# A dilated convolution with gates on one NeuronCore: short groups moved to the end, wide blocks re-spaced, preparation in smaller pieces

## The chip, the core and the metric

The kernel runs on one core of one Trainium2 chip. The metric is the time of one execution on the device in microseconds; the median of three runs of the kernel before is 282.95 (282.88 to 283.25). The engines of the core run their own queues side by side: TensorE (matmuls, PE in the profile), VectorE (DVE), ScalarE (ACT), GpSimd (POOL), and SyncE (SP), which here issues most transfers. Matmuls write to PSUM; GpSimd works on SBUF alone.

## The reference

```python
B, T, D, K = (2, 16000, 256, 3)
xp = jnp.pad(x, ((0, 0), (pad, 0), (0, 0)))      # dil = 2, pad = 4
h = jnp.einsum('btc,cd->btd', xp[:, pad:pad + T, :], w[0])
for i in range(1, K):
    off = pad - i * dil
    h = h + jnp.einsum('btc,cd->btd', xp[:, off:off + T, :], w[i])
f = h[..., :D].copy()
g = h[..., D:].copy()
z = jnp.tanh(f) * _sigmoid(g)
return z @ w_o
```

Each time step takes its input and those of 2 and 4 steps earlier through three 256 x 512 matrices; half of the result goes through tanh, half through a sigmoid, and their product through a 256 x 256 projection. Everything is bfloat16.

## The kernel before

**Rows and groups.** Four time steps make a row, so a batch has 4000 rows. A transposed load (L128) puts channels on the 128 partitions: `xt` holds, for each of the four steps of a row and for both halves of the channels, the rows side by side. Rows are cut into *groups* of R rows: 256 in most, and where a batch does not divide, 160 and 128 at its end (batch 0: 160 and 128; batch 1: 160, 128 and 128) and 128 at the start of batch 0. One or two groups share a loaded *chunk*. In the kernel before the groups stand batch after batch, so the two short ones of batch 0 are groups 12 and 13 of 28, in the middle.

**Blocks.** A group has four *blocks*, one for each 128 of the 512 output columns (`O_ORDER`; two for tanh, two for the sigmoid; `oi` is 0 to 3). The convolution is done with fewer products than its taps would need: sums and differences of inputs (`mm` L278, `pp` L284, `dd` L295) are multiplied with sums and differences of the weights (`wm`, `wp`, `wd`), four pairs of matmuls to a block (L314), and sums behind them (L348, L349) put the two halves right in the PSUM banks `a` and `b`.

**Wide blocks.** Three stretches of 256 rows in each batch go another way, with eight steps to a row and seven pairs of matmuls of 256 columns (L227) in place of four pairs of 512. That is less work for TensorE and more for the others: extra copies by ScalarE (L241, L242), four sums by VectorE (L247 twice, L257, L258), operands `qa`, `qb`, `qd` by GpSimd (L199, `wide_part`, six parts of 512 elements), `qp` (L214) and `qm` (L222). Six wide units of four blocks are put between the plain ones. They need three more weight matrices (`wf`, `wu`, `wt`), which VectorE makes in twelve steps (L571), and wide unit 0's operands, which GpSimd makes in twelve half parts ahead of it. The operands of unit n + 1 are made during the blocks of unit n (`Q_PARTS`).

**The order.** The order on every engine is written out: `slots` lists the 136 blocks, and the loop over k issues, for block k: on TensorE the first two products of block k, the last two of block k - 1, then projection pieces (`out_mm`, L413); on ScalarE the copy `ss` of one bank (L342), the eviction of earlier pieces (L450, L435) and the activations of block k - 1 (L372, L362); on VectorE the sums of block k, then one operation for `mm`, `pp` or a gate `zz` (L389), then what preparation is due; on GpSimd one part of `dd` for the next group, then a piece of the wide operands. `after` makes GpSimd's operations wait for VectorE's last one. For a wide block the products are `wide_first`, `wide_second` and `wide_last` (the last in block k + 1).

**Pieces.** A finished group's gated values go through the projection in *pieces* of four matmuls (`pieces`: 4 for a group of 256 rows or a wide unit, 3 for 160, of which one is a small `odd` one, 2 for 128). `drain` puts them on the list `todo`, from which each block takes one; behind the last wide block every second block takes two while there are more pieces left than blocks. A block that finds the list empty has none.

**Where the wide blocks stand** (the number is the block k; unit and `oi` run in order):

| | unit 0 | unit 1 | unit 2 | unit 3 | unit 4 | unit 5 |
|---|---|---|---|---|---|---|
| before | 40 43 46 49 | 63 66 69 72 | 75 78 81 84 | 87 90 93 96 | 99 102 105 108 | 111 114 117 120 |
| after | 34 36 46 52 | 57 60 63 66 | 69 71 75 78 | 81 83 86 89 | 92 95 98 101 | 104 106 109 112 |

Before, the weight steps are in blocks 9, 11, ... 31 and the half parts in 12, 14, ... 34; `qp` and `qm` of unit 0 in blocks 35 and 37. Short groups are blocks 52 to 59 and 124 to 135 before, 116 to 135 after.

Of the kernel before, what the change touches and what calls it, by code (L numbers as in the profile page):

```python
# [9 lines left out]
ALU = mybir.AluOpType  # L10
# [3 lines left out]
def kernel(  # L14
# [19 lines left out]
    nc = tc.nc  # L34
    bf16 = mybir.dt.bfloat16
    f32 = mybir.dt.float32
    B, T, D = x.shape
    K, _, D2 = w.shape
    P = 128
    assert K == 3 and D % P == 0 and D2 == 2 * D and T % 64 == 0  # L40
    CT = D // P
    NT = D // P
    RH = 16
    RG = 256
    N_WARM = 14
    O_ORDER = (0, 2, 1, 3)
# [2 lines left out]
    LAST = ((128,), (128, 128))  # L49
    N_DIRECT = 4  # L50
    N_WIDE = (3, 3)
    WIDE_FROM = 40
    PREP = 28
    W_FROM = 9
    EVERY = (2,)
    W_POOL = ()
    SUM_POOL = True
    GATE2 = False
    Q_PARTS = ((0, 1), ("s", 2), (3, 4), (5,))
    SPLIT_PROJ = 1  # L60
    W_STEP = 2
    P_STEP = 2
# [7 lines left out]


    groups, chunks, wides = [], [], []
    for b in range(B):
        r0 = 0
        wide = N_WIDE[min(b, 1)]
        head, tail = sizes(FIRST if b == 0 else (), LAST[min(b, 1)], wide)
        cuts = [1, 1] if b == 0 else []
        for rs in (head, tail):
            i = 0
            while i < len(rs):  # L80
                n = cuts.pop(0) if cuts else 2
                part = rs[i:i + n]
                chunks.append((b, r0, sum(part), len(groups), len(part)))
                for r in part:
                    groups.append(dict(wide=False, b=b, r0=r0, R=r, chunk=len(chunks) - 1, col=r0 - chunks[-1][1]))
                    r0 += r
                i += n
            if rs is head:
                assert r0 > 0 and r0 % 2 == 0
                for _ in range(wide):  # L90
                    wides.append(dict(wide=True, b=b, r0=r0, R=P))
                    r0 += RG
    XW = max(c[2] for c in chunks)

    consts = ctx.enter_context(tc.tile_pool(name="consts", bufs=1))
# [40 lines left out]
    w_taps = [consts.tile([P, CT, D2], bf16, name=f"w{k}_sb") for k in range(K)]  # L136
# [19 lines left out]
    wf_sb = consts.tile([P, CT, D2], f32)  # L156
    wu_sb = consts.tile([P, CT, D2], bf16)
    wt_sb = consts.tile([P, CT, D2], bf16)
# [24 lines left out]
            in_=x[G["b"], t0 - 8 * RH:t0 + 8 * P, :].rearrange("(r j) c -> r (j c)", j=8),  # L183
        )

    def wide_part(n, part, behind=None, qs=slice(0, 2)):

        G = wides[n]
        c = [G["x"][:, 2 * i:2 * i + 2, :, RH:RH + P] for i in range(4)]
        e = [G["x"][:, 2 * i:2 * i + 2, :, RH - 1:RH - 1 + P] for i in range(4)]  # L190
        if part == 0 and qs.start == 0:
            for nm in ("qa", "qb", "qd"):
                G[nm] = q_pool.tile([P, 2, 2, CT, P], bf16, name=nm)
        nm, h, in0, in1, op = (
            ("qa", 0, c[0], c[2], ALU.add), ("qb", 0, e[3], c[1], ALU.add),
            ("qa", 1, c[2], c[0], ALU.subtract), ("qb", 1, e[3], c[1], ALU.subtract),
            ("qd", 0, e[2], c[2], ALU.subtract), ("qd", 1, c[3], e[3], ALU.subtract),
        )[part]
        after(nc.gpsimd.tensor_tensor(out=G[nm][:, h, qs], in0=in0[:, qs], in1=in1[:, qs], op=op), behind)  # L199

    def gates(G):
        if GATE2 and G["R"] % P == 0:
# [6 lines left out]

    def wide_sum(n, behind=None):  # L210
        G = wides[n]
        G["qp"] = q_pool.tile([P, 2, CT, P], bf16, name="qp")
        eng = nc.gpsimd if SUM_POOL and behind else nc.vector
        ins = eng.tensor_tensor(out=G["qp"][:], in0=G["qa"][:, 0], in1=G["qb"][:, 0], op=ALU.subtract)  # L214
        if eng is nc.vector:
            return ins
        after(ins, behind)

    def wide_diff(n):
        G = wides[n]  # L220
        G["qm"] = q_pool.tile([P, 2, 2, CT, P], bf16, name="qm")
        return nc.vector.tensor_tensor(out=G["qm"][:], in0=G["qa"][:], in1=G["qb"][:], op=ALU.add)  # L222

# [6 lines left out]
            )  # L230

    def wide_first(G, oi):
        for bank, pool in (("a", ps_a), ("b", ps_b)):
            G[bank, oi] = pool.tile([P, 2 * RG], f32, name=bank)
        wide_mm(G, oi, wm_sb, G["qp"], "a", 1, True)
        wide_mm(G, oi, w_taps[1], G["qm"][:, 1], "a", 0)
        wide_mm(G, oi, wp_sb, G["qm"][:, 0], "b", 1, True)

    def wide_copies(G, oi):
        G["ss", oi] = ss_pool.tile([P, RG], f32, name="sw")  # L240
        nc.scalar.mul(G["ss", oi][:], G["a", oi][:, RG:], 0.5)  # L241
        nc.scalar.mul(G["a", oi][:, RG:], G["a", oi][:, :RG], -1.0)  # L242

    def wide_sums(G, oi):
        G["ud", oi] = ud_pool.tile([P, 2, RG], f32, name="ud")
# [5 lines left out]
    def wide_second(G, oi):  # L251
        wide_mm(G, oi, wt_sb, G["qa"][:, 1], "a", 0)
        wide_mm(G, oi, wu_sb, G["qb"][:, 1], "a", 1)
# [4 lines left out]
        nc.vector.tensor_tensor(out=G["a", oi][:], in0=ud, in1=G["a", oi][:], op=ALU.add)  # L258

    def wide_last(G, oi, bank):  # L260
        if bank == "b":
            wide_mm(G, oi, wd0_sb, G["qd"][:, 1], "b", 1)
        else:
            wide_mm(G, oi, wd2_sb, G["qd"][:, 0], "a", 0)

    def after(ins, behind):
        if behind is not None:
            tc.add_manual_dep(
                ins.ins, behind.ins.name,
                mybir.DependencyInfo(mybir.DependencyClass.Sync, mybir.DependencyReason.DATA),  # L270
                reason="GpSimd reads SBUF while VectorE's sums read PSUM",
            )
# [223 lines left out]
    NG = len(groups)  # L496
    plain = [(False, g, oi) for g in range(NG) for oi in range(4)]
    rest = [(True, n, oi) for n in range(len(wides)) for oi in range(4)]
    slots, since = [], 0
    for i, (_, g, oi) in enumerate(plain):  # L500
        slots.append(plain[i])
        since += 1
        full = all(groups[plain[j][1]]["R"] == RG for j in range(max(i - 2, 0), min(i + 2, len(plain))))
        if rest and i + 1 >= WIDE_FROM and since >= EVERY[(4 * len(wides) - len(rest)) % len(EVERY)] and full:
            slots.append(rest.pop(0))
            since = 0
    assert not rest
    NB = len(slots)
# [6 lines left out]
    todo, made = [], []  # L515
# [33 lines left out]
    for part in range(4):  # L549
        last = pre_d(1, part, nc.vector)  # L550
# [6 lines left out]
    drain(groups[0], N_DIRECT + 2)  # L557


    extra = {}  # L560
    last_wide = max(k for k in range(NB) if slots[k][0])
    first_wide = slots.index((True, 0, 0))

    def weight_steps(oi):
        o = O_ORDER[oi]
        osl = slice(o * P, (o + 1) * P)
        eng = nc.gpsimd if oi in W_POOL else nc.vector

        def tt(out, in0, in1, op):
            def step(last):  # L570
                ins = eng.tensor_tensor(out=out[:, :, osl], in0=in0[:, :, osl], in1=in1[:, :, osl], op=op)  # L571
                if eng is nc.vector:
                    return ins
                after(ins, last)
                return last
            return step

        return [
            tt(wf_sb, w_taps[2], w_taps[0], ALU.subtract),
            tt(wu_sb, wf_sb, w_taps[1], ALU.add),  # L580
            tt(wt_sb, wf_sb, w_taps[1], ALU.subtract),
        ]

    steps = [s for oi in range(4) for s in weight_steps(oi)]
    ks = [k for k in range(N_DIRECT + 2, NB) if not slots[k][0]]
    for kk, s in zip([kk for kk in ks if kk >= W_FROM][::W_STEP], steps):
        extra.setdefault(kk, []).append(s)

    load_wide(0)
    wides_loaded = 1  # L590
    wide_parts = {first_wide - PREP + P_STEP * i: divmod(i, 2) for i in range(12)}

    held = []
    filled = None
# [1 line left out]
    k = N_DIRECT + 1  # L596
    while k <= NB:
# [3 lines left out]
        if k < NB:  # L601
            if w:
                wide_first(G, oi)
                wide_copies(G, oi)
            else:
                products(k, 2)
                products(k, 1)
                copy_m2(k)
# [5 lines left out]
        if not prev["wide"]:  # L614
            products(k - 1, 3)
            products(k - 1, 0)
        if k < NB:
            for piece in made:
                out_evict(*piece, (not w and g == NG - 1 and oi in (0, 2)) or (len(made) > 1 and piece is made[1]))
            made = []  # L620
        second = (lambda: wide_second(G, oi)) if w else (lambda: wide_last(prev, poi, "b")) if prev["wide"] else None
        n = 0 if k in (NB - 2, NB - 1) else 2 if k > last_wide + 3 and k % 2 and unmade > NB - 1 - k else 1
        while todo and todo[0][0] <= k and n:
            piece = todo.pop(0)[1]
            out_mm(*piece, between=second)
# [51 lines left out]
        if k == last_wide + 2:  # L677
            last = gates(wides[-1])
            drain(wides[-1], k + 2)
        if k == first_wide - 5:  # L680
            last = wide_sum(0)
        if k == first_wide - 3:
            last = wide_diff(0)

        for step in extra.get(k, ()):
            last = step(last)
        if k < NB and g + 1 < NG:
            filled = last or filled
            if k + 1 < NB and slots[k + 1][0]:
                held.append(lambda last2, args=(g + 1, oi, nc.gpsimd), last1=last: pre_d(*args, last2 or last1))  # L690
            else:
                pre_d(g + 1, oi - 1 if g == 1 else oi, nc.gpsimd, last)
        if k in wide_parts:
            part, q = wide_parts[k]
            wide_part(0, part, last, slice(q, q + 1))
        if k < NB:
            activate(k - 1)
        if k < NB and oi == 3 and loaded < len(chunks) and groups[min(g + 1, NG - 1)]["chunk"] + 2 >= loaded:
# [3 lines left out]
                load_wide(1)  # L702
                wides_loaded = 2
        k += 1
    assert not todo, len(todo)
    finish(made)


# [28 lines left out]
```

## Time and profile before

| | us |
|---|---|
| median of three runs | 282.95 |
| profiled execution, its time | 282.88 |
| its span on the profile | 281.1 |
| TensorE busy | 275.2 |
| VectorE busy | 262.1 |
| ScalarE busy | 260.5 |
| GpSimd busy | 148.8 |
| projection, L413 out of `zz`, 392 matmuls | 63.5 |
| `dd` on GpSimd, L295, 103 in all | 99.4, and 110.3 of idle time before them |

Busy time counts an instruction from its start to the end of its writing, and instructions that follow each other on an engine overlap, so the distance from start to start tells what one costs: of VectorE's sums of 512 columns the mean is about 690 ns, the distance 600. The projection pieces and blocks can be told in the timeline by their tiles: a plain block begins with the pair `b<-mm`, a wide one with `a<-qp`, a piece is four matmuls `o_ps`. The granted clock of TensorE is 1.00 in every stretch but the last.

### The profile page before, as it was taken

How to read it: one execution, taken by the hardware profiler on the slowest of the kernel's cores; microseconds unless marked ns; L12 is line 12 of the kernel's file. 1: busy time of each engine (PE TensorE's matmuls, PEld its weight loads, DVE VectorE, ACT ScalarE, POOL GpSimd, SP SyncE). 2: the span in 40 equal slices, each digit the busy share in tenths (PEclk: the TensorE clock that was granted, in tenths of full speed). 3: DMA queues.
4: the chain of work that ended last, by engine and by line, in shares of the span. 5: the costliest groups of instructions: out<-in, count | busy, mean ns of one | idle time of the engine just before them, and what ended most of it. 6: DMA issues, size and time to landing. Idle time of an engine off the chain costs nothing.

```text
span 281.1 us, 5263 instructions
## 1 busy us (share of the span) xinstructions
PE 275.2 (98%) x1770; PEld 172.4 (61%) x1770; DVE 262.1 (93%) x477; ACT 260.5 (93%) x553; POOL 148.8 (53%) x160
## 2 busy tenths in 40 slices
PE   8999999999999999999999999999999999999994
PEld 6544555555556665765665666666666666666883
DVE  3999999999999999899999999999999999999994
ACT  5798999999999998999999999999999999999984
POOL 1145756677656663366664766575476553223320
PEclk9999999999999999999999999999999999999999
DMA  8999292642516319536269019515711711222333
GB/s 211 241 192 240 83 219 76 146 123 75 127 75 157 109 45 186 158 119 160 76 137 216 37 40 240 147 40 131 183 40 75 163 40 75 84 74 78 113 124 111
DMA packets 77979, 34.88 MB, mean 124 GB/s; under 512 B 68224, under 2 KB 70144, under 8 KB 77952
## 3 DMA queue, kind: packets, MB, share of 16 engines
q1 hardware_dynamic: 76992, 33.82, 47.4%
q10 hardware_dynamic: 960, 0.72, 0.8%
q8 instruction: 14, 0.23, 0.4%
q14 instruction: 13, 0.11, 0.1%
HBM read 1.18 MB, written 16.38 MB: 62 GB/s over the span
## 4 chain that ended last, share of the span: by engine, by line
PE 92%; DVE 4%; ACT 2%; issue 1%; DVEq 0%
PE b L314 29%; PE a L314 28%; PE o_ps L413 19%; PE a L227 9%; PE b L227 4%; PE a L115 1%; PE a L332 1%; PE b L332 1%; DVE b L348 1%; DVE b L257 1%; DVE a L349 1%; ACT ss L342 1%; ACT thw L362 0%; ACT th L372 0%; DVE mm L278 0%
## 5 line engine op out<-in xcount | busy, mean ns | idle before, releaser
L295 POOL TENSOR_TENSOR dd<-xt 128x512 bf16<-128x512 bf16 (+2 forms) x103 | 99.4, 965 | 110.3 <-DVE zz L389 41.9
L348 DVE TENSOR_TENSOR b<-a,ss 128x512 f32<-128x512 f32 (+2 forms) x108 | 70.0, 649 | 3.7 <-ACT ss L342 1.5
L349 DVE TENSOR_TENSOR a<-a,ss 128x512 f32<-128x512 f32 (+2 forms) x108 | 69.4, 642 | 0.0
L342 ACT COPY ss<-b 128x512 f32<-128x512 f32 (+2 forms) x108 | 60.3, 558 | 9.3 <-PE b L314 2.1
L314 PEld LDWEIGHTS <-wd_sb 128*128 128x128 bf16 x432 | 41.8, 98 | 40.0 <-issue 1.5
L413 PE MATMUL o_ps<-wo_sb,zz 128*128 128x256 bf16 x392 | 63.5, 272 | 0.0
L314 PE MATMUL b<-dd,wd_sb 128*128 128x512 bf16 (+2 forms) x216 | 60.4, 361 | 0.1
L314 PE MATMUL a<-dd,wd_sb 128*128 128x512 bf16 (+2 forms) x216 | 60.4, 361 | 0.0
L314 PE MATMUL a<-pp,wp_sb 128*128 128x512 bf16 (+2 forms) x216 | 60.4, 361 | 0.0
L314 PE MATMUL b<-mm,wm_sb 128*128 128x512 bf16 (+2 forms) x216 | 60.4, 361 | 0.0
L450 ACT CAST osb<-o_ps 128x512 bf16<-128x512 f32 x92 | 55.1, 599 | 0.0
L413 PEld LDWEIGHTS <-zz 128*128 128x128 bf16 x392 | 38.3, 98 | 22.2
L389 DVE TENSOR_TENSOR zz<-th,sg 128x1024 bf16<-128x1024 bf16 (+1 forms) x55 | 37.1, 677 | 0.0
L314 PEld LDWEIGHTS <-wp_sb 128*128 128x128 bf16 x216 | 21.0, 98 | 21.9 <-DVE pp L284 0.7
L372 ACT ACTIVATE sg<-b 128x512 bf16<-128x512 f32 (+2 forms) x56 | 33.0, 589 | 0.9 <-PE b L332 0.5
L372 ACT ACTIVATE th<-b 128x512 bf16<-128x512 f32 (+2 forms) x56 | 32.2, 575 | 1.6 <-PE b L314 0.8
L372 ACT ACTIVATE sg<-a 128x512 bf16<-128x512 f32 (+2 forms) x56 | 33.1, 591 | 0.0
L372 ACT ACTIVATE th<-a 128x512 bf16<-128x512 f32 (+2 forms) x56 | 32.4, 578 | 0.0
L314 PEld LDWEIGHTS <-wm_sb 128*128 128x128 bf16 x216 | 21.0, 97 | 3.5
L257 DVE TENSOR_TENSOR b<-ud,a 128x512 f32<-128x512 f32 x24 | 16.7, 696 | 5.9 <-PE a L227 3.8
L284 DVE TENSOR_TENSOR pp<-xt 128x1024 bf16<-128x1024 bf16 (+2 forms) x27 | 18.2, 673 | 0.0
L247 DVE SCALAR_TENSOR_TENSOR ud<-b,sw 128x256 f32<-128x256 f32 x48 | 17.9, 414 | 0.2
(74 smaller groups left out, 331.2 us busy)
## 6 DMA issues: line engine op xcount, KB each, us to landing
out_dram<-osb SPq DMA_DIRECT2D x60, 256.0 KB, 2.1
w_sb<-in_w_dram ACTq DMA_DIRECT2D x2, 256.0 KB, 4.2
out_dram<-osb_end SPq DMA_DIRECT2D x3, 128.0 KB, 1.9
xn<-in_x_dram SPq DMA_DIRECT2D x1, 256.0 KB, 3.0
w_sb<-in_w_dram SPq DMA_DIRECT2D x1, 256.0 KB, 4.1
xt<-in_x_dram SPq DMA_TRANSPOSE x15, 6.7
wo_sb<-in_w_o_dram ACTq DMA_DIRECT2D x1, 128.0 KB, 5.1
out_dram<-osb_odd SPq DMA_DIRECT2D x8, 16.0 KB, 2.0
```

The costliest lines, as they stand in the source:

```text
L227: nc.tensor.matmul(G[bank, oi][:, half * RG:(half + 1) * RG], lhsT=wmat[:, ct, o * P:(o + 1) * P], rhs=mv[:, :, ct, :], start=first and ct ...
L257: nc.vector.tensor_tensor(out=G["b", oi][:], in0=ud, in1=G["a", oi][:], op=ALU.subtract)
L284: return nc.vector.tensor_tensor(out=G["p"][:, :, :, :G["R"]], in0=xc, in1=yp, op=ALU.add)
L295: ins = eng.tensor_tensor(out=G["d"][:, j, :, :R], in0=a[:, q], in1=s[:, q], op=ALU.subtract)
L314: nc.tensor.matmul(G[bank, oi][:, :N], lhsT=wmat[:, ct, osl], rhs=mv(ct), start=first and ct == 0, stop=ct == CT - 1, skip_group_check=True,)
L342: nc.scalar.copy(out=G["ss", oi][:, :N], in_=G["b", oi][:, :N])
L348: nc.vector.tensor_tensor(out=pb[:, :N], in0=pa[:, :N], in1=ss[:, :N], op=ALU.subtract)
L349: nc.vector.tensor_tensor(out=pa[:, :N], in0=pa[:, :N], in1=ss[:, :N], op=ALU.add)
L372: nc.scalar.activation(out=dst[:, 2 * h:2 * h + 2, :R], in_=G[bank, oi][:, :2 * R].rearrange("p (q r) -> p q r", q=2), func=func, scale=1. ...
L389: return nc.vector.tensor_tensor(out=G["z"][:, dt, :, :full], in0=G["th"][:, dt, :, :full], in1=G["sg"][:, dt, :, :full], op=ALU.mult)
L413: nc.tensor.matmul(o_ps[:, q, :], lhsT=lhsT, rhs=wo_sb[:, dt, :], start=(dt == 0), stop=(dt == NT - 1),)
L450: copy(out=osb[:, 2 * jp:2 * jp + 2, :], in_=o_ps[:])
```

## The change

Short groups of both batches stand at the end (`SHORT_LAST`): the groups of 160 and 128 rows of batch 0 come behind all groups of 256 rows of both batches. The distances of the wide blocks are written out one by one (`SPACING`, in plain blocks). The twelve weight steps and the 24 quarters of unit 0's six parts have their blocks written out (`W_AT`, two halves to a step; `P_AT`, four quarters to a part); halves or quarters of one block are joined where they lie side by side. One weight step (`W_ENG`) is made by GpSimd. `SUM_AT` and `DIFF_AT` place `qp` and `qm`. Only block 128 takes two pieces (`TWICE`). `wide_copies` is called behind the last products of the block before, still ahead of the evictions. `HOLD`, `EVICT_DVE` and `COPIES` are empty or 0.

```diff
-    WIDE_FROM = 40
-    PREP = 28
-    W_FROM = 9
-    EVERY = (2,)
-    W_POOL = ()
+    SPACING = (34, 1, 9, 5, 4, 2, 2, 2, 2, 1, 3, 2, 2, 1, 2, 2, 2, 2, 2, 2, 2, 1, 2, 2,)
+    W_ENG = (0, 0, 0, 0, 0, 0, 0, 1, 0, 0, 0, 0)
+    W_AT = (6, 6, 10, 10, 13, 14, 15, 16, 17, 17, 21, 21, 24, 24, 24, 26, 27, 29, 30, 32, 40, 42, 42, 45)
+    P_AT = (8, 10, 10, 11, 12, 13, 14, 17, 17, 18, 19, 19, 24, 24, 26, 27, 28, 31, 31, 31, 31, 31, 33, 33)
+    SUM_AT, DIFF_AT = 22, 31
+    HOLD = ()
+    TWICE = (128,)
+    COPIES = 0
+    EVICT_DVE = ()
     SUM_POOL = True
+    SHORT_LAST = True
...
+        add_groups(b, head, [1, 1] if b == 0 else [])
+        assert starts[b] > 0 and starts[b] % 2 == 0
+        for _ in range(wide):
+            wides.append(dict(wide=True, b=b, r0=starts[b], R=P))
+            starts[b] += RG
+        ends.append(tail)
+        if not SHORT_LAST or b == B - 1:
+            for e in range(b + 1 if SHORT_LAST else 1):
+                add_groups(e if SHORT_LAST else b, ends[e if SHORT_LAST else b])
...
-        if rest and i + 1 >= WIDE_FROM and since >= EVERY[(4 * len(wides) - len(rest)) % len(EVERY)] and full:
+        if rest and since >= SPACING[4 * len(wides) - len(rest)] and full:
...
-    for kk, s in zip([kk for kk in ks if kk >= W_FROM][::W_STEP], steps):
-        extra.setdefault(kk, []).append(s)
+    for i, kk in enumerate(W_AT):
+        extra.setdefault(kk, []).append((i // 2, i % 2))
+
+    def weight_step(i, cts, last):
+        o = O_ORDER[i // 3]
+        sl = (slice(None), cts, slice(o * P, (o + 1) * P))
+        out, in0, in1, op = (
+            (wf_sb, w_taps[2], w_taps[0], ALU.subtract),
+            (wu_sb, wf_sb, w_taps[1], ALU.add),
+            (wt_sb, wf_sb, w_taps[1], ALU.subtract),
+        )[i % 3]
+        assert i % 3 == 0 or w_made.get(3 * (i // 3)) == CT
+        w_made[i] = w_made.get(i, 0) + cts.stop - cts.start
+        eng = nc.gpsimd if W_ENG[i] else nc.vector
+        ins = eng.tensor_tensor(out=out[sl], in0=in0[sl], in1=in1[sl], op=op)
+        if W_ENG[i]:
+            after(ins, last)
+            return last
+        return ins
...
-    wide_parts = {first_wide - PREP + P_STEP * i: divmod(i, 2) for i in range(12)}
+    wide_parts = {}
+    for i, kk in enumerate(P_AT):
+        wide_parts.setdefault(kk, []).append((i // 4, i % 4))
...
                 wide_first(G, oi)
-                wide_copies(G, oi)
+                if COPIES == 1:
+                    wide_copies(G, oi, (0,))
...
+            if w and COPIES == 0:
+                wide_copies(G, oi)
             for piece in made:
-                out_evict(*piece, (not w and g == NG - 1 and oi in (0, 2)) or (len(made) > 1 and piece is made[1]))
+                out_evict(*piece, (not w and g == NG - 1 and oi in (0, 2)) or (len(made) > 1 and piece is made[1]) or k in EVICT_DVE)
...
-        n = 0 if k in (NB - 2, NB - 1) else 2 if k > last_wide + 3 and k % 2 and unmade > NB - 1 - k else 1
+        n = 0 if k in (NB - 2, NB - 1) or k in HOLD else 2 if k in TWICE else 1
...
-        if k == first_wide - 5:
+        if k == SUM_AT:
             last = wide_sum(0)
-        if k == first_wide - 3:
+        if k == DIFF_AT:
             last = wide_diff(0)
...
+        todo_parts = wide_parts.pop(k, [])
+        for part in sorted({part for part, _ in todo_parts}):
+            qc = sorted(i for p, i in todo_parts if p == part)
+            if len(qc) == 4:
+                wide_part(0, part, last)
+            elif len(qc) == 2 and qc[0] % 2 == 0:
+                wide_part(0, part, last, slice(qc[0] // 2, qc[0] // 2 + 1))
+            else:
+                for i in qc:
+                    wide_part(0, part, last, slice(i // 2, i // 2 + 1), slice(i % 2, i % 2 + 1))
```

## The prediction

> **What bounds the kernel now.** I read the page first: the engines' busy shares and the shares of the chain that ended last.
>
> ```profile
> PE 275.2 (98%) x1770; PEld 172.4 (61%) x1770; DVE 262.1 (93%) x477; ACT 260.5 (93%) x553; POOL 148.8 (53%) x160
> ...
> PE 92%; DVE 4%; ACT 2%; issue 1%; DVEq 0%
> ```
>
> TensorE is the chain; the count of its instructions does not change, so only the time in which it stands still can be won. VectorE and ScalarE follow at 93%, close enough to be the cause wherever it does stand still. Next the windows, over three stretches.
>
> ```profile
> core 0: us, PE busy (x) PEld busy (x) DVE busy (x) ACT busy (x) POOL busy (x), PEclk, DMA share, GB/s
> 26.00:70.00 44.00, 44.00 (x245) 23.75 (x244) 43.73 (x72) 41.66 (x82) 29.59 (x31) 1.00 0.50 127
> ...
> 111.00:122.50 11.50, 11.50 (x95) 8.97 (x93) 10.56 (x25) 11.50 (x32) 5.25 (x7) 1.00 0.56 153
> ```
>
> From 26 to 70 us, where the weights and the first wide block's operands are prepared, VectorE has no room (43.73 of 44.00) and TensorE is still fed. In the short groups in the middle ScalarE is the full one (11.50 of 11.50). Third, the timeline of TensorE: the distance from one block's first matmul to the next one's is the block's length. An undisturbed block of 256 rows takes 2.16 us with one projection piece and 1.73 without; a wide block 2.39 and 1.96; a plain block right behind a wide one 1.74 with a piece, so about 1.74 - 0.43 = 1.31 without. Against these:
>
> ```profile
> 149.43 0.59 PE L314 MATMUL b<-mm,wm_sb 128*128 128x512 bf16 x2
> 149.86 0.59 PE L314 MATMUL a<-pp,wp_sb 128*128 128x512 bf16 x2
> 150.35 0.38 PE L227 MATMUL b<-qd,wd_sb 128*128 128x256 bf16 x2
> 150.95 0.38 PE L227 MATMUL a<-qd,wd_sb 128*128 128x256 bf16 x2 [0.22 <-DVE a L258]
> 151.17 0.59 PE L314 MATMUL b<-mm,wm_sb 128*128 128x512 bf16 x2
> ```
>
> This is block 73, 1.74 us long where 1.31 would do: 0.43 lost. It has no projection piece, and TensorE waits for the sums (L257, L258) that VectorE forms for wide block 72 before it. Four sums' starts in a row (.60 apart) show that a plain block costs VectorE 3 x 0.60 = 1.80 us, a wide one with a gate or `qm` 4 x 0.60 + small = 2.47; a block without a piece is too short for that. The same reading finds: block 11, 2.57 for 2.16 (0.41); 49 and 50, 2.31 for 1.96 and 2.21 for 1.74 (0.35 + 0.47); 64, 2.01 for 1.74 (0.27); 76, 2.17 for 1.74 (0.43); 97, 2.09 for 1.74 (0.35); the short blocks 55, 56, 59 some 0.18 together; the short blocks 126 to 132 about 0.32; 29, 31, 33 about 0.1. Blocks 49, 50, 64, 73 and 76 lie in or just behind a shortage of pieces (48, 49, 62, 73, 74 have none, 61 half a one).
>
> **The change, part by part.** (A) *Order.* With the short groups of batch 0 no longer in the middle, groups 11 and 12 are both 256 rows and pieces come four to a group. I followed the list of pieces through the new order: from block 55 to 133 every block has one. Without one are, behind the start, 39, 40, 49 and 54, all plain, each followed by two plain blocks or by one with a piece. Lag of VectorE there: at 39 and 40 (1.80 - 1.73) + (2.00 - 1.73) = 0.34, then the next block gives 0.36 back. What lag is free: a block's second pair of matmuls ends 1.02 us into it (149.86 + 0.59 - 149.43), its first sum 0.69 later at 1.71, and that is used at 1.73 + 0.87 = 2.60 at the earliest, so 0.8 or more. Hence 49, 50 (-0.82), 64, 73, 76 (-1.13) go: -1.95. Block 97's 0.35 has a piece and the same neighbours as undisturbed block 85; I can't name its cause and leave it (bounds 0 and -0.35).
>
> (B) *Twenty short blocks at the end.* A block of 128 rows, timeline:
>
> ```profile
> 118.44 0.38 PE L314 MATMUL b<-mm,wm_sb 128*128 128x256 bf16 x2
> ...
> 118.91 0.37 ACT L342 COPY ss<-b 128x256 f32<-128x256 f32 x1
> ...
> 119.17 0.59 ACT L450 CAST osb<-o_ps 128x512 bf16<-128x512 f32 x1
> ...
> 119.65 0.40 ACT L372 ACTIVATE th<-b 128x256 bf16<-128x256 f32 x1
> 119.75 0.38 PE L314 MATMUL b<-mm,wm_sb 128*128 128x256 bf16 x2
> 119.93 0.41 ACT L372 ACTIVATE th<-a 128x256 bf16<-128x256 f32 x1
> ...
> 120.22 0.38 ACT L342 COPY ss<-b 128x256 f32<-128x256 f32 x1
> ```
>
> TensorE 119.75 - 118.44 = 1.31; ScalarE, start to start, .26 + .48 + .28 + .29 = 1.31, without a gap: even. VectorE needs 4 rows of 0.33 less overlap, about 1.05. Today's mid blocks 57 and 58 lose nothing so; the old tail, with pieces in pairs, loses 0.07 in most blocks; the new one has one piece each but for block 128. Blocks of 160 rows: TensorE 1.52, ScalarE .32 + .66 + .48 = 1.46. Today 0.18 + 0.32 = 0.50; for the new tail I take 0.25, between none and the old tail's 0.07 x 20 = 1.4: -0.25. The last four blocks and the finish are the same instructions.
>
> (C) *Weights and wide operands.* GpSimd's pieces meet VectorE's operations that read SBUF twice:
>
> ```profile
> 43.24 0.62 POOL L199 TENSOR_TENSOR qb<-xq 128x256 bf16<-128x256 bf16 x1
> ...
> 43.28 1.13 DVE L389 TENSOR_TENSOR zz<-th,sg 128x1024 bf16<-128x1024 bf16 x1
> ...
> 44.33 0.41 DVE L571 TENSOR_TENSOR wt_sb<-wf_sb,w_sb 128x256 bf16<-128x256 f32 x1
> ```
>
> The gate `zz`, 0.60 from start to start elsewhere, holds VectorE 44.33 - 43.28 = 1.05: 0.45 lost per piece; ten of the twelve pieces show 0.37 to 0.49, on `zz` or on the weight step. Blocks 12 to 33, before: 22 x 1.80 + 10 weight steps x 0.335 + 11 x 0.45 = 47.9 us of VectorE against 22 x 2.165 = 47.6 of TensorE: full, as the window says, at a loss of 0.1. After: 39.6 + 8 half steps x 0.20 (half of 0.335 plus about 0.03, estimate) + 3 whole x 0.335 + `qp` 0.34 + `qm` 0.60 = 43.1, so 4.5 us of room for 18 GpSimd pieces (16 of `wide_part`, 2 of the weights). What a quarter piece costs no row shows. Its length, from GpSimd's 1.04 us at 512 elements and 0.61 at 256, is some 0.40; a half piece costs its length less 0.17, so a quarter some 0.22 (nothing, if it ends before VectorE's next SBUF operation; 0.45 at worst, the whole of a half piece's price). 18 x 0.22 = 4.0: it fits, with little left. I take +0.2 for uneven blocks (31 issues four pieces, so 32 has about 2.5 us for VectorE). The pieces sit behind `dd` on GpSimd's queue; the `dd` that is wanted soonest, of a block with oi 3, goes ahead of them and has some 2 us. Bounds: -0.1 and, at 0.45, 18 x 0.45 - 4.5 = +3.6.
>
> The Trainium skill ("SBUF — State Buffer", SBUF: two separate sides) says that a VectorE operation with two SBUF inputs and a GpSimd operation exclude each other for the whole instruction of whoever is first. By that, `zz` above would lose the 0.58 us that were left of the piece; the trace has 0.45, and a quarter would cost 0.36, 18 of them 6.5, 2.0 over the room. I keep the measured relation.
>
> (D) *Start.* VectorE has no gap from 19.05 to 25 us, and block 11 waits for block 10's sums (start 23.33, TensorE at 24.07). The weight step of block 9 goes (-0.335), one at block 6 comes (+0.335, of which 0.18 falls into the gap before 19.05), the quarter piece of block 8 may hold block 9's `zz` 0.2 to 0.35, block 10 gets a whole step and two pieces, which block 12 takes with 0.5 to spare. I take +0.1, bounds -0.2 and +0.6. The wide input lands at 16.0 us, before block 8.
>
> (E) *Close wide blocks* (34/36, 69/71, 81/83, 104/106, one plain block between). Both pairs of blocks together: ScalarE 2 x (2.15 + 1.92) = 8.14, VectorE 7.94 at most, TensorE 2 x (2.38 + 1.74) = 8.24. The second one's negated copy (L242) would end about 1.6 us into it, its user comes at 1.74. I take +0.15 for the four, bounds 0 and 4 x 0.4 = 1.6, what 64 or 76 lost. The moved `wide_copies` keeps its place on ScalarE's queue: nothing. Output and input transfers keep their count and their place relative to groups; those of SyncE's queue run groups ahead.
>
> Sum: -1.95 - 0.25 + 0.2 + 0.1 + 0.15 = -1.75. The profiled execution's 281.1 us of span and 1.78 around it make 282.88; less 1.75 is 281.1. The median shown is 282.95, 0.07 above, nothing at this precision.
>
> **Rivals.** 1. *Close wide blocks stall* (E at its bound, 1.6): -1.75 + 1.45 = -0.3, 282.6. For it: ScalarE's 0.1 us of margin in such a pair. Against: it gains 0.2 us on TensorE in each wide block.
> 2. *The start gives back* (D at 0.6, C at 0.5 in the next blocks): 282.88 - 1.75 + 0.8 = 281.9. For it: no slack before 25 us.
> 3. *VectorE becomes the bound from block 12 to 33: slower.* Mechanism: what a meeting costs is the handover and not the piece's length, so twice as many pieces cost twice as much. At 0.45 each, +3.6 in place of +0.2: 282.88 - 1.95 + 3.6 = 284.5. It makes the kernel slower from (4.5 + 1.95) / 18 = 0.36 per piece on. For it: the `zz` of 43.28 lost 0.45 to a piece that ran 0.58 beyond its start, and 0.37 to 0.49 came of all of them. Against: quarter pieces may end before VectorE has finished the two sums that run beside them. (The exclusion in the Trainium skill's page gives 0.36, just the break-even.)
> 4. *ScalarE bounds the tail*: 0.07 to 0.1 lost in each of 20 blocks, 1.4 to 2: 282.5. For it: 11.50 of 11.50. Against: blocks 57 and 58.
>
> **How the numbers follow.** Forecast 0.60, rival 1 0.10, 2 0.13, 3 0.11, 4 0.06. The time is that of the forecast, 281.1. Its own bounds: all gains and no cost, -1.95 - 0.5 - 0.2 - 0.1 - 0.35 = -3.1, 279.8; with rivals 2 and part of 1 and 4, 282.4; rival 3 is left out. Range 279.9 to 282.4. About 0.2% (0.57 us) is what a measurement here can tell from no change: faster by more is the forecast, rival 2 and a little of 1 and 4, 0.80; within it the rest of 1 and 4, 0.08; slower rival 3 with a share of mishaps, 0.12.
>
> **What would show it.** No TensorE wait before `b<-qd` or `a<-qd` behind wide blocks from 52 to 112; block lengths 1.31 and 1.52 in the tail; block 11 at most 0.4 too long; VectorE's `zz` beside quarter pieces at 0.8 from start to start, not 1.05. Wrong if blocks 12 to 33 exceed 2.16 on the average, or the tail's exceed 1.4.

## The result and the profile after

| | before | after |
|---|---|---|
| median, us | 283.07 (282.88 to 283.25, 4 runs) | 280.34 (280.19 to 280.74, 4 runs) |
| profiled execution, its time | 282.88 | 280.25 |
| its span | 281.1 | 278.5 |
| last matmul begins at | 277.01 | 274.56 |

The ratio after to before is 0.9906 with a 95% interval of 0.9888 to 0.9923: 2.7 us faster by the medians, 2.63 by the two profiled executions. The forecast was 281.1, its range 279.9 to 282.4.

The page of after: first the busy time of the engines, then the shares of the chain that ended last.

```profile
PE 273.7 (98%) x1770; PEld 173.6 (62%) x1770; DVE 259.8 (93%) x479; ACT 260.9 (94%) x556; POOL 152.5 (55%) x170
...
PE 98%; DVE 0%; DVEq 0%; issue 0%
```

TensorE had 92% of the chain before and has 98% now. VectorE's 4% and ScalarE's 2%, which were the waits for sums and copies, are gone. The instruction counts say the same as the diff: TensorE has as many as before, GpSimd ten more, because its preparation is cut finer.

The windows of after, over the preparation stretch and over a stretch of the tail where all blocks have 160 or 128 rows:

```profile
core 0: us, PE busy (x) PEld busy (x) DVE busy (x) ACT busy (x) POOL busy (x), PEclk, DMA share, GB/s
26.00:70.00 44.00, 44.00 (x245) 23.83 (x244) 43.30 (x75) 41.69 (x82) 31.93 (x37) 1.00 0.48 128
250.00:261.50 11.50, 11.50 (x99) 9.51 (x98) 9.81 (x27) 11.50 (x34) 5.32 (x8) 1.00 0.25 93
```

From 26 to 70 us VectorE is nearly as full as before (43.30, it was 43.73): the finer pieces won little room there. In the tail ScalarE is full (11.50 of 11.50), as it was in the middle of the kernel before, and TensorE goes on without a gap. Full and just even costs nothing.

As in the prediction, a block is taken from its first matmul to the next block's, and what it is longer than an undisturbed block of its kind is its lost time. Summed by stretch:

| blocks | before | after | what changed |
|---|---|---|---|
| 4 to 11 | 1.17 | 0.35 | blocks 4, 5: 0.57 to 0; block 11: 0.41 to 0.08 |
| 12 to 33 | 0.26 | 0.17 | |
| 34 to 115 | 3.26 | 1.30 | 49, 50, 64, 73, 76: 2.01 to 0; 97: 0.36 to 0; 56, 59: 0.18 to 0; 35 and 37: 0 to 0.62 |
| 116 to 134 | 0.56 | 0.17 | |

The first row is no gain. Block 4 began at 9.71 us before and at 10.53 after, and block 12 at 25.54 and 25.53: what was lost in the one run within these blocks was lost in the other ahead of them. The other rows, 0.09 + 1.96 + 0.39 = 2.44, are the 2.45 us by which the last matmul comes sooner. The undisturbed lengths are rounded down, so a sum over many blocks comes out some tenths high, before and after alike: in after no single block from 12 to 33 lost anything that can be read, and from 34 to 115 only 35 and 37 lost 0.05 or more.

The one new loss is at 35 and 37, the plain blocks behind the close wide blocks 34 and 36. The timeline of TensorE in after, from the start of block 35 to that of block 36's first products:

```profile
75.53 0.59 PE L336 MATMUL b<-mm,wm_sb 128*128 128x512 bf16 x2
75.96 0.59 PE L336 MATMUL a<-pp,wp_sb 128*128 128x512 bf16 x2
76.39 0.38 PE L435 MATMUL o_ps<-wo_sb,zz 128*128 128x256 bf16 x2
76.81 0.39 PE L243 MATMUL b<-qd,wd_sb 128*128 128x256 bf16 x2
77.03 0.38 PE L435 MATMUL o_ps<-wo_sb,zz 128*128 128x256 bf16 x2
77.40 0.38 PE L243 MATMUL a<-qd,wd_sb 128*128 128x256 bf16 x2
77.61 0.38 PE L243 MATMUL a<-qp,wm_sb 128*128 128x256 bf16 x2
```

A pair of matmuls of 256 columns (x2) takes 0.22 from start to start. So `b<-qd` could have begun at 76.61 and began 0.20 later; `a<-qd` could have begun at 77.25 and began 0.15 later. They add to banks that the sums L278 and L279 write first. VectorE and then GpSimd, in the same run:

```profile
71.55 0.91 DVE L300 TENSOR_TENSOR mm<-xt 128x1024 bf16<-128x1024 bf16 x1
72.38 0.48 DVE L601 TENSOR_TENSOR wf_sb<-w_sb 128x128 f32<-128x128 bf16 x1
72.79 0.69 DVE L370 TENSOR_TENSOR b<-a,ss 128x512 f32<-128x512 f32 x1
73.39 0.68 DVE L371 TENSOR_TENSOR a<-a,ss 128x512 f32<-128x512 f32 x1
73.98 1.30 DVE L411 TENSOR_TENSOR zz<-th,sg 128x1024 bf16<-128x1024 bf16 x1
75.20 0.74 DVE L268 SCALAR_TENSOR_TENSOR ud<-b,sw 128x256 f32<-128x256 f32 x2
76.05 0.70 DVE L278 TENSOR_TENSOR b<-ud,a 128x512 f32<-128x512 f32 x1
76.66 0.69 DVE L279 TENSOR_TENSOR a<-ud,a 128x512 f32<-128x512 f32 x1
```

```profile
71.51 2.19 POOL L213 TENSOR_TENSOR qd<-xq 128x128 bf16<-128x128 bf16 x4
...
73.70 1.03 POOL L317 TENSOR_TENSOR dd<-xt 128x512 bf16<-128x512 bf16 x1
```

`mm` takes 0.83 from start to start where 0.60 is usual, because it meets the quarter pieces; the weight step adds 0.41; `zz` takes 1.22, because the `dd` that waited behind the pieces of `qd` (the row x4: three quarters and a half) begins 0.28 ahead of it. VectorE is 0.23 + 0.41 + 0.62 = 1.26 behind, and its sums end just as late as TensorE's waits show (76.05 + 0.70 = 76.75, then 76.81; 76.66 + 0.69 = 77.35, then 77.40).

### The profile page after: what moved, and what is told of

The parts are those of the page before. It is cut to its first block, busy times and chain, and to the rows that moved or that the text cites. A ratio compares the mean times of both kernels' runs of the same rounds, so it can differ in the third digit from the quotient of the medians.

```text
span 278.5 us, 5278 instructions
## 1 busy us (share of the span) xinstructions
PE 273.7 (98%) x1770; PEld 173.6 (62%) x1770; DVE 259.8 (93%) x479; ACT 260.9 (94%) x556; POOL 152.5 (55%) x170
## 4 chain that ended last, share of the span: by engine, by line
PE 98%; DVE 0%; DVEq 0%; issue 0%
PE a L336 31%; PE b L336 31%; PE o_ps L435 19%; PE a L243 10%; PE b L243 4%; PE a L354 1%; PE a L128 1%; PE b L354 1%; PE tp L180 0%; DVE osb_end L505 0%; PE b L498 0%; DVEq L766 0%; PE a L498 0%; DVE warm L148 0%
## 5 line engine op out<-in xcount | busy, mean ns | idle before, releaser
L435 PE MATMUL o_ps<-wo_sb,zz 128*128 128x256 bf16 x392 | 64.5, 273 | 0.0
L472 ACT CAST osb<-o_ps 128x512 bf16<-128x512 f32 x95 | 57.1, 601 | 0.0
L411 DVE TENSOR_TENSOR zz<-th,sg 128x1024 bf16<-128x1024 bf16 (+1 forms) x55 | 36.3, 662 | 0.0
L278 DVE TENSOR_TENSOR b<-ud,a 128x512 f32<-128x512 f32 x24 | 16.7, 696 | 4.0 <-PE a L243 2.1
L300 DVE TENSOR_TENSOR mm<-xt 128x1024 bf16<-128x1024 bf16 (+2 forms) x27 | 17.8, 659 | 0.3 <-DMA xt<-in_x_dram 0.3
```

The lines of the kernel that those rows point to most:

```text
L300: return nc.vector.tensor_tensor(out=G["m"][:, :, :, :G["R"]], in0=xc, in1=yp, op=ALU.subtract)
L411: return nc.vector.tensor_tensor(out=G["z"][:, dt, :, :full], in0=G["th"][:, dt, :, :full], in1=G["sg"][:, dt, :, :full], op=ALU.mult)
L435: nc.tensor.matmul(o_ps[:, q, :], lhsT=lhsT, rhs=wo_sb[:, dt, :], start=(dt == 0), stop=(dt == NT - 1),)
L472: copy(out=osb[:, 2 * jp:2 * jp + 2, :], in_=o_ps[:])
```

## The experiments

Twelve runs; "lost" is lost time by blocks, as above. Times are medians of several runs, but for the last two kernels, which ran once. The kernel before, run beside each of them, had medians of 283.12 to 283.23 (283.07 in the result), so times from different rounds compare to some 0.2.

**Before, with a piece held back ahead of wide blocks.** Does a missing piece next to a wide block cost time, and how much?

```diff
-        n = 0 if k in (NB - 2, NB - 1) else ...
+        n = 0 if k in (NB - 2, NB - 1) or k in (38, 42, 45, 65, 68) else ...
```

> The kernel before, with nothing moved but projection pieces: blocks 38, 42, 45, 65 and 68 take none, so that 43, 48, 49, 73 and 74, which had none, have one. Theory (a block without a piece in or behind a wide block is too short for VectorE): the losses of 49, 50, 73 and 76 go, 0.8 + 0.8 us, and the blocks that gave their piece lose nothing; about 281.4. Rival (these waits come of something else at those places, the preparation of the next wide unit or the transfers): the losses stay, 283.

Measured: 282.34 (10 runs) against 283.16, ratio 0.9972 (0.996 to 0.9985). The losses of 49, 50, 73 and 76 are gone, as expected, but new ones came at the blocks that gave up a piece directly *ahead* of a wide one (42, 45, 68): 43 0.19, 46 0.19, 47 0.27, 69 0.19, 70 0.27. Block 47 on TensorE in this run:

```profile
100.78 0.60 PE L314 MATMUL a<-pp,wp_sb 128*128 128x512 bf16 x2
101.21 0.38 PE L413 MATMUL o_ps<-wo_sb,zz 128*128 128x256 bf16 x2
101.53 0.38 PE L227 MATMUL b<-qd,wd_sb 128*128 128x256 bf16 x2
101.74 0.38 PE L413 MATMUL o_ps<-wo_sb,zz 128*128 128x256 bf16 x2
102.13 0.38 PE L227 MATMUL a<-qd,wd_sb 128*128 128x256 bf16 x2
```

`b<-qd` is 0.10 late and `a<-qd` 0.17, although block 47 has its piece: the debt was made two blocks earlier. Blocks 38 and 65 gave up theirs at no cost, although 65 too stands directly ahead of a wide block (66); why it got by is not shown. Blocks 34 to 115 lose 2.63 in place of 3.26, so the expectation was met by less than half. A short block can cost on *either* side of a wide block. Block 64, behind 62 without and 61 with half a piece, still loses 0.29.

**After, with one piece moved away from block 79**, which follows wide block 78.

```diff
-    HOLD = ()
-    TWICE = (128,)
+    HOLD = (79,)
+    TWICE = (116, 128)
```

> The changed kernel with no piece in block 79, right behind wide block 78; block 116 takes two. Theory: 79 is 1.74 us long where 1.31 would do, a wait of about 0.4 for VectorE's sums, so 0.3 to 0.5 slower than the changed kernel. Rival (what is lost there is slack that later blocks give back): no change of the whole, under 0.15.

Measured: 280.81 (280.53 to 280.96). Block 79 on TensorE in this run, up to the next block's first products:

```profile
167.28 0.60 PE L336 MATMUL b<-mm,wm_sb 128*128 128x512 bf16 x2
167.71 0.59 PE L336 MATMUL a<-pp,wp_sb 128*128 128x512 bf16 x2
168.21 0.38 PE L243 MATMUL b<-qd,wd_sb 128*128 128x256 bf16 x2
168.80 0.38 PE L243 MATMUL a<-qd,wd_sb 128*128 128x256 bf16 x2 [0.22 <-DVE a L279]
169.02 0.59 PE L336 MATMUL b<-mm,wm_sb 128*128 128x512 bf16 x2
```

Block 79 loses 0.45, as much as 73 and 76 before, and nothing else moved (34 to 115: 1.76 for 1.30). One piece less in the wrong place is 0.45 us. With the run above, in which pieces given back took the losses away, this shows the cause at 49, 50, 73 and 76. Block 64 was never given its pieces by themselves.

**After, with the first close pair opened** (wide blocks 34 and 37).

```diff
-    SPACING = (34, 1, 9, 5, 4, ...
+    SPACING = (34, 2, 8, 5, 4, ...
```

> The changed kernel with the first two wide blocks two plain blocks apart in place of one (34 and 37). Theory (GpSimd's pieces of blocks 31 to 34 hold VectorE, and the closeness of the wide blocks is not it): block 35 still loses 0.3, the block behind the second wide one less than the 0.25 it loses now; 0.1 to 0.3 faster. Rival (the closeness does it): both losses go, 0.6 faster.

Measured: 280.73 (280.16 to 280.96), ratio 0.9911 (0.9889 to 0.9933). Block 35 still loses 0.36; the second loss shrinks from 0.26 to 0.06 + 0.04. So of the 0.62 only some 0.2 comes of the closeness; the rest was there already, whatever follows block 35. In the time the 0.2 is not to be seen.

**After, with the last twelve quarter pieces spread** over blocks 20 to 30 rather than five of them in block 31.

```diff
-    P_AT = (..., 24, 24, 26, 27, 28, 31, 31, 31, 31, 31, 33, 33)
+    P_AT = (..., 20, 21, 22, 23, 24, 25, 26, 27, 28, 29, 30, 30)
```

> The changed kernel with the last twelve quarter parts at blocks 20 to 30, one each (two at 30), in place of 24 to 33 with five quarters at 31. Theory (GpSimd's burst holds VectorE): block 35's 0.35 goes and block 37's 0.25 goes or halves, blocks 20 to 33 stay at 2.16; 0.35 to 0.6 faster. Rival (closeness): 35 and 37 lose as before, no change; if VectorE has no room in 20 to 30, some tenths slower.

Measured: 280.83 (279.78 to 281.11). The losses at 35 and 37 are gone, and block 33 loses 0.65 in their place (12 to 33: 0.81 for 0.17). So the burst alone is not the cause. Spread, the pieces met VectorE oftener: from 47 to 71 us nine of its operations `mm`, `pp` and `zz` took 0.91 to 1.12 where 0.68 is usual, in after three, 0.78 to 0.91. The windows, first of after, then of this run:

```profile
26.00:72.00 46.00, 46.00 (x256) 24.91 (x255) 45.30 (x78) 43.60 (x85) 33.42 (x40) 1.00 0.50 132
```

```profile
26.00:72.00 46.00, 46.00 (x256) 24.74 (x253) 45.84 (x76) 43.49 (x85) 35.49 (x45) 1.00 0.50 126
```

VectorE is busy for 45.84 of 46.00 here and for 45.30 in after. Whether some placing does without a loss is open: after leaves VectorE 0.70 us of this stretch, and no run filled it.

**After, with half pieces and whole weight steps** in the even manner of before, early enough for a wide block at 34.

```diff
+    W_ENG = (0,) * 12
+    W_AT = (9, 9, 11, 11, 13, 13, 15, 15, 17, 17, 19, 19, 21, 21, 23, 23, 25, 25, 27, 27, 29, 29, 31, 31)
+    P_AT = (8, 8, 10, 10, 12, 12, 14, 14, 16, 16, 18, 18, 20, 20, 22, 22, 24, 24, 26, 26, 28, 28, 30, 30)
+    SUM_AT, DIFF_AT = 29, 31
```

> The changed kernel's order of blocks with the preparation in the old grain: twelve half parts at blocks 8, 10, ... 30, twelve whole weight steps on VectorE at 9, 11, ... 31, the sum and difference of unit 0 at 29 and 31. Theory (a meeting costs VectorE by the piece's length, 0.45 for a half part and about 0.23 for a quarter, and there is no room for the former once the first wide block is at 34): blocks 12 to 33 lose 0.6 to 1.7 us in place of 0.2, 0.7 to 1.5 slower than the changed kernel. Rival (the grain does not matter): within 0.3 of it.

Measured: 282.1 (10 runs) against 283.12, ratio 0.9966 (0.9953 to 0.9979). Blocks 4 to 11 lose 1.12, 12 to 33 1.79, 34 to 115 1.04. The windows of this run:

```profile
core 0: us, PE busy (x) PEld busy (x) DVE busy (x) ACT busy (x) POOL busy (x), PEclk, DMA share, GB/s
26.00:72.00 46.00, 45.96 (x251) 23.86 (x250) 46.00 (x74) 42.80 (x83) 30.63 (x32) 1.00 0.45 118
```

VectorE is busy for all of 46.00. The finer preparation is worth 282.1 - 280.34 = 1.8 us here, but only because the first wide block comes six blocks earlier: with the old deadline the half pieces lost 0.26 there.

**Before with the new order of groups alone** (wide blocks from 40, two plain blocks between; old preparation, old rule for pieces).

```diff
     SHORT_LAST = True
+    SPACING = (40, 2, 2, ...)
+    n = 0 if ... else 2 if k > last_wide + 3 and k % 2 and unmade > NB - 1 - k else 1
```

> The kernel before with the order of groups alone changed (short groups of both batches last): first wide block at 40, then one behind every second plain block, preparation in the old grain and places. Blocks 43, 48 and 49 have no piece, later ones have. Theory: what 64, 73, 76 lost and the short blocks in the middle is gone, what 49 and 50 lost (0.8) stays, the tail loses at most 0.2: 1.5 to 2.0 less lost than before, 281.2 to 281.7. Rival (the finer preparation brings the time): within 0.5 of before.

Measured: 281.28 (281.1 to 281.71), ratio 0.9936 (0.9917 to 0.9956). The losses of 64, 73, 76, 97 and of the middle are gone; 49 and 50 keep 0.36 and 0.49, since their blocks 43, 48 and 49 are short of pieces as before; the tail is worse, 1.11 for 0.56. (This kernel keeps the place that `wide_copies` has in after.) What the finer preparation is worth beside the new order is open: no run has the new order and the even tail with the old preparation and a spacing that keeps wide blocks away from 43, 48 and 49. Without the 0.85 of 49 and 50 and the 0.94 that the tail loses above after's, this kernel would lose, from block 12 on, some 0.4 to 0.5 us less than after; that is an estimate from the lost times above.

**After with the short groups back in the middle** and the old rule for two pieces in a block.

```diff
-    SHORT_LAST = True
+    SHORT_LAST = False
...
-        n = 0 if ... else 2 if k in TWICE else 1
+        n = 0 if ... else 2 if k > last_wide + 3 and k % 2 and unmade > NB - 1 - k else 1
```

> The changed kernel with the short groups of batch 0 back in the middle (blocks 53 to 60), wide blocks at 34, 36, 46, 62, 67, 70, ... and pieces in pairs at the end as before. No piece in 61, 64, 65, 66. Theory: 62, 63 and 67, 68 lose 0.3 to 0.9 together for want of a piece ahead of the wide block, the short blocks 0.2, the tail 0.4 more: 0.9 to 1.5 slower than the changed kernel. Rival (order is of no weight): within 0.3.

Measured: 281.58 (281.25 to 281.92), 1.24 more than after: 63 loses 0.29, 67 0.16, 68 0.45, the tail 0.71 for 0.17. So the move of the groups (with its spacing of the wide blocks) is worth 1.2 to 1.8 of the 2.7, seen from either end: 1.24 when it is taken back together with the even tail, 1.8 when it is made alone under the old rule.

**After with later first wide blocks** (38, 41, 47, 52), quarter pieces spread to block 36 and all weight steps on VectorE, from block 17 on whole.

```diff
+    SPACING = (38, 2, 5, 4, 4, ...)
+    W_ENG = (0,) * 12
+    W_AT = (..., 21, 21, 25, 25, 29, 29, 37, 37, 40, 40, 45, 45, 50, 50)
+    P_AT = (..., 24, 24, 26, 27, 28, 30, 32, 33, 34, 35, 36, 36)
```

> The changed kernel with the first wide unit at 38, 41, 47 and 52 (the rest unmoved), the last ten quarter parts at 26 to 36, none above two in a block, and eight half weight steps moved to blocks from 29 to 50. Theory (35 and 37 lose to a VectorE that has had 2.4 to 2.5 us of work in blocks 31 and 32): with four more blocks' room nothing above 0.15 is lost from 12 to 50, 0.4 to 0.6 faster than the changed kernel, 279.8 to 280.0. Rival (whatever stands ahead of the first two wide blocks, they lose it): no change.

Measured: 280.09 (279.57 to 280.45), ratio 0.9891 (0.9869 to 0.9912). 35 and 37 lose nothing; 48 loses 0.26 behind the weight step of block 45. 34 to 115: 1.02 for 1.30.

**The same with that weight step at block 43**, beside **after itself once more** on the same chip.

```diff
-    W_AT = (..., 45, 45, 50, 50)
+    W_AT = (..., 43, 43, 50, 50)
```

> The kernel after with its first wide blocks at 38, 41, 47 and 52, the quarter pieces spread over blocks 8 to 36, and the tenth weight step at block 43 in place of 45. Theory (VectorE falls behind where extra work meets a wide block; the stall of block 48 in the version with that step at 45 came from it): blocks 35, 37 and 48 lose nothing, blocks 34 to 115 lose 0.7 to 0.8 together against 1.30, and it is 0.4 to 0.6 us faster than the kernel after in the same call, about 279.8. Rival (the lost time only moves to another block): 34 to 115 lose 1.0 or more, no difference from after that can be told.

> The kernel after, unchanged, beside the version before it in this call: 280.2 to 280.7, for a comparison on the same chip.

Measured: 280.1 (280.01 to 280.98) and 280.18 (280.08 to 280.85), five runs each; before had 283.23. Block 48 is free, but 45 and 53 now lose 0.21 each (34 to 115: 1.09). My theory fell and the rival held: the debt moves on. With a later first wide block 0.2 to 0.3 us of the lost time can be had in the trace, and that is less than the times can tell.

**After with two pieces in a block by the old rule** (117, 119 and 131 take two, 130 and 133 none).

```diff
-        n = 0 if ... else 2 if k in TWICE else 1
+        n = 0 if ... else 2 if k > last_wide + 3 and k % 2 and unmade > NB - 1 - k else 1
```

> The kernel after with the old rule for two pieces in a block behind the last wide one: blocks 117, 119 and 131 take two and 130 and 133 none, in place of 128 taking two. Theory (a short block loses when pieces come unevenly): 0.27 to 0.45 in each of blocks 131 to 133, as in the version of the kernel before with the new order of groups, where these three lost 1.0; blocks 117 and 119 are plain ones of 128 or 160 rows and lose 0.1 to 0.3 each; blocks 116 to 134 lose 0.9 to 1.3 in place of 0.17, and the time is some 281.2. Rival (the tail of the version of the kernel before was late for another reason): below 0.4 in blocks 116 to 134, time as after.

Measured: 280.62, one run. Blocks 131 to 133 lose 0.19, 0.29 and 0.41, blocks 116 to 134 1.11 in all for 0.17; 117 and 119 cost less than expected (0.07 and 0.05 in the blocks behind them). The end of block 131 on TensorE, then blocks 132 and 133:

```profile
267.31 1.04 PE L435 MATMUL o_ps<-wo_sb,zz 128*128 128x256 bf16 x8
268.18 0.38 PE L336 MATMUL b<-mm,wm_sb 128*128 128x256 bf16 x2
268.40 0.38 PE L336 MATMUL a<-pp,wp_sb 128*128 128x256 bf16 x2
268.62 0.38 PE L336 MATMUL b<-dd,wd_sb 128*128 128x256 bf16 x2
268.83 0.38 PE L336 MATMUL a<-dd,wd_sb 128*128 128x256 bf16 x2
269.33 0.38 PE L435 MATMUL o_ps<-wo_sb,zo 128*128 128x256 bf16 x2
269.55 0.38 PE L336 MATMUL b<-mm,wm_sb 128*128 128x256 bf16 x2
269.77 0.38 PE L336 MATMUL a<-pp,wp_sb 128*128 128x256 bf16 x2
270.27 0.39 PE L336 MATMUL b<-dd,wd_sb 128*128 128x256 bf16 x2
```

The piece behind block 132 begins 0.28 late (268.83 + 0.22 = 269.05) and the last products of block 132, issued within 133, 0.28 late as well (269.77 + 0.22 = 269.99). The time is 0.44 above the median of after beside it and only 0.09 above that one's profiled execution (280.53): block 12 began 0.57 sooner here (25.01, 25.58), the last matmul comes 0.38 later (274.98, 274.60), which 0.94 - 0.57 = 0.37 fits, and what follows it took 0.21 less (3.85, 4.06). The even pieces of the tail are thus a part of the gain of their own by lost time; one run's time can't show it.

**Before with VectorE's stream shifted**: eight small operations behind the first one, for the 0.36 of block 97 that the prediction could not name.

```diff
     nc.vector.memset(warm[:], 0.0)
+    spare = consts.tile([P, 1], bf16)
+    for _ in range(8):
+        nc.vector.memset(spare[:], 0.0)
```

> The kernel before with eight small VectorE operations put in at the start, so that every later one stands eight places further back in VectorE's stream. Theory (the 0.36 lost in block 97 hangs on a place in the stream): block 97 loses nothing, or the loss stands two blocks earlier, in block 95. Rival (it hangs on what blocks 94 to 97 do): block 97 loses 0.36 as before. The time is that of before within 0.3 either way.

Measured: 282.94, one run. VectorE at blocks 96 and 97, in before:

```profile
199.10 0.75 DVE L247 SCALAR_TENSOR_TENSOR ud<-b,sw 128x256 f32<-128x256 f32 x2
200.30 0.70 DVE L257 TENSOR_TENSOR b<-ud,a 128x512 f32<-128x512 f32 x1 [0.46 <-PE o_ps L413]
```

and in this kernel (three lines further down in the file):

```profile
199.02 0.74 DVE L250 SCALAR_TENSOR_TENSOR ud<-b,sw 128x256 f32<-128x256 f32 x2
199.87 0.70 DVE L260 TENSOR_TENSOR b<-ud,a 128x512 f32<-128x512 f32 x1
```

The gap is gone, block 97 loses nothing, every other loss of the middle stands where it stood (49, 50, 64, 73, 76), and no new one of this size came. What blocks 94 to 97 do is the same, and in the run with pieces held back, where VectorE's stream was not shifted, block 97 lost its 0.36 as before. So the loss seems to hang on where the instructions stand in the program and not on the work; that rests on one profile of the shifted kernel. Why it does so is not shown; a gap of the same form (0.45 ahead of the same sum) stood at block 70 of the kernel with half pieces, and nowhere in after.

## Why the prediction was right, and where not

**What bounds the kernel** held: TensorE is the chain, and 2.45 of the 2.63 us are its lost time.

**(A), -1.95.** Right in place and size: 49, 50, 64, 73 and 76 lost 2.01 and lose nothing now; 39, 40, 49 and 54, which have no piece now, lose nothing either, since none stands beside a wide block. The run with block 79 short shows the cause at 0.45. The reading was too narrow in one point: it spoke of shortage in or behind a wide block, and the runs show it ahead of one too, at three blocks of four. And the name *Order* took in too much: with the order alone 49 and 50 still lose 0.85, so that part of the 2.01 comes of where the first wide blocks stand and not of the short groups. Block 97's 0.35 was left at nothing and came in full: -0.36, by luck and no merit of the change, as the shifted stream suggests.

**(B), -0.25.** The mechanism was right and the size too small: the middle and the tail together went from 0.18 + 0.56 to 0.17, -0.57. The blocks stand at 1.31 and 1.52 us as worked out. Most of the error is in the old tail: it was read as 0.32, from blocks 126 to 132, and is 0.56 from 116 to 134, which makes 0.24 of the 0.32 missed. The other 0.08 is the new tail, put at 0.25; blocks 57 and 58, which lost nothing at one piece each, were the nearer row.

**(C), +0.2.** A quarter piece was put at 0.22 us of VectorE. Measured, with the quarter pieces of `qa` ahead of `zz` in after:

```profile
26.66 1.26 POOL L213 TENSOR_TENSOR qa<-xq 128x128 bf16<-128x128 bf16 x2
...
26.70 0.93 DVE L411 TENSOR_TENSOR zz<-th,sg 128x1024 bf16<-128x1024 bf16 x1
...
27.56 0.69 DVE L370 TENSOR_TENSOR b<-a,ss 128x512 f32<-128x512 f32 x1
```

From `zz` to the next sum it is 0.86, so some 0.25 over the usual 0.60; three more meetings cost 0.23 to 0.24, and in others it was GpSimd that waited. As a total "it fits, with little left" held: VectorE stood idle for 0.70 us from 26 to 72 us, and blocks 12 to 33 lost 0.09 *less* than before. Some luck is in it. Four of the 16 pieces that I counted as quarters, in blocks 19, 24, 31 and 33, are two quarters joined; at the price of a half the sum is 4 x 0.45 + 14 x 0.22 = 4.9, more than the room of 4.5. In the trace none of the four held VectorE: two began behind its operation and waited, two ran beside its sums in PSUM. What failed is the end of the stretch. I priced meetings with the pieces alone, and the costliest was with a `dd` that four pieces of block 31 had pushed late: 0.62 of `zz` at 73.98. VectorE came out of block 33 in debt and paid behind it; with the pair opened it still paid 0.36 + 0.06 + 0.04. So the term is some 0.4, and it fell on other blocks than I thought.

**(D), +0.1.** Even, 25.54 and 25.53 at block 12. Over all runs block 12 began at 25.42 to 25.73 with the old preparation (four profiles) and at 24.91 to 25.84 with the new (nine), so 0.1 either way can't be told. Block 11 is 0.08 too long, well inside "at most 0.4".

**(E), +0.15.** This step was wrong in its reason. I spread the cost over four close pairs and named ScalarE's margin of 0.1 us. Three pairs cost nothing; the first cost 0.62, and VectorE was late, not ScalarE. Only some 0.2 of it is due to the closeness (the opened pair), the rest belongs to (C). The test that I gave, no wait before `b<-qd` or `a<-qd` from block 52 on, left out the very pair in which it failed.

**Sum.** 2.63 came against 1.75: 0.36 + 0.06 more from (A), 0.32 from (B), 0.29 from (C)'s own blocks, 0.10 from (D), 0.17 behind the last matmul, less 0.47 at (E), which is 0.83 of the 0.88. The 0.17 is chance: what follows the last matmul takes 3.84 to 4.66 us in the profiles of all runs.

**The rivals.** 1 came at one pair in four and at 0.62 of its 1.6, and only some 0.2 of that is closeness. 2 did not come. 3, that a meeting costs the handover and not the length, is out: 0.23 to 0.25 for a quarter against 0.45 for a half, below the 0.36 at which it would have made the kernel slower. The forms of before at the new deadline (the run with half pieces) come nearest to it. 4 did not come, though ScalarE is full: 1.31 us is enough.

## What to carry to other kernels

Where several engines are nearly full, a piece of filler for TensorE (here four projection matmuls) that is missing beside a block heavy for VectorE can cost its whole length (0.45 us here, though wide block 43 of before and block 65 of the run with pieces held back, short as well, cost under 0.05), while one missing among light blocks (39, 40, 49 and 54 of after) cost nothing: place the filler by the neighbours, not by counts. When the debt of an engine only moves as its work is moved (35 and 37, then 33, then 45, 48 and 53), count the engine's meetings, and take work off it or move the deadline. Before a loss is put down to the code around it, shift the instruction stream by a few empty operations and see if it stays.

## What the runs showed of the hardware

A VectorE operation with two operands in SBUF that starts behind a GpSimd operation is held, as a rule, for what is left of that operation less about 0.13 us. Three meetings, from start times and lengths of the profiles: `zz` at 43.28 in before, 0.58 left of `qb`, 0.45 lost; `zz` at 73.98 in after, 0.75 left of `dd`, 0.62 lost; `zz` at 26.70, some 0.37 left of a quarter of 0.40 to 0.43, 0.25 lost. Twice in after it went the other way: `zz` at 22.73 began 0.04 behind a quarter of `qa` and lost nothing, and the quarter took 1.01; `pp` at 41.43 began 0.05 behind a quarter of `qb`, which took 0.99. So the start times of the profile do not always tell which of the two waits. The Trainium skill ("SBUF — State Buffer", SBUF: two separate sides) says that the loser waits for the whole instruction of the winner. The traces agree but for that constant; for a quarter piece it is a third of the price, which is why 0.25 was lost there and not 0.36.

The record of the full granted clock begins 3.75 to 7.09 us into the span, and not by kernel: after alone had 6.44 and 6.53, its version with pairs in the tail, equal at the start, 3.75. (The windows, which give 1.00 from 0 us on, count the time ahead of that record as full.) Ahead of it matmuls are slower: from the first six, `a<-xt`, to the next it took 1.23 us in after (4.99 to 6.22) and 0.66 in that version (4.72 to 5.38). Block 12 began at 25.01 us in that version against 25.53 and 25.58. The clock is not all of it: with the same preparation up to there, block 12 began at 25.31 where the record began at 3.77 (the opened pair) and at 24.91 where it began at 5.14 (the short groups back in the middle). Half a microsecond between single executions can so be nothing but the start. The Trainium skill ("TensorE: Matmul & The Clock Gate", Part 1: The HAM clock gate) says that the clock follows a free-running window of activity, so that the ramp differs from run to run; the traces agree. That page's 500 ns either way for the transition is too little for them: 3.34 us lie between the earliest and the latest.
